# Batches 2 to 5 of a fused attention and expert kernel get new slots, and two product phases are interleaved

## The chip, the cores and the metric

The kernel runs on one core of one Trainium2 chip. The metric is the device time of one execution in microseconds (us), lower is better. PE is TensorE, ACT is ScalarE, DVE is VectorE, POOL is GpSimd and SP is SyncE.

## What is computed

Attention with a causal window of 64 positions over 8 batches and 8 heads of 576 positions and 64 dimensions, then two matrix products with `h - tanh(h)` between them.

```
scores = q @ k^T / sqrt(64);  mask = (0 <= i - j < 64)
attn   = softmax(where(mask, scores, -1e9)) @ v
x      = attn, heads side by side: [4608 tokens, 512]
h      = x @ w_in                  # [4608, 2048]
out    = (h - tanh(h)) @ w_out     # [4608, 512], float32
```

## The kernel before, in words

**Attention.** A batch b has four pairs of heads, numbered g = 4b to 4b+3. Each pair has nine tiles j of 64 queries and 128 keys. Its steps are these:

- `load` and `load_all` (lines 97 and 103) bring q and k from DRAM on POOL's queue, as one pair or as all eight heads of a batch; `load_v_all` (146) brings V into `vall`, of which there is one buffer.
- `cast` (86) brings a pair's rows into the order that PE takes, on DVE or POOL, in three row buffers each for q and k. `tr` (267) transposes them on PE through PSUM bank 3. For q, ACT copies one half out and then DVE the other; for k, ACT copies all of it.
- `scores` (334) makes three tiles in PSUM bank 4, and ACT takes the exponential (336). `masking` (340, DVE) sets the hidden part to zero. In batches 0 and 1 `tile_scores` (306) and `tile_pv` (322) do it for 64-column halves.
- `cast_v` (86) puts V into `vb`, of which there is one buffer. `keys_v` and `windows_v` (176, 161) move it to `vw`, nine DMAs for a batch, each of which a tile j needs.
- `tile_pv` (20 matmuls of 65 columns, banks 6 and 7; 322 to 328) or `pv` with `norm` (9 matmuls of 130 columns, banks 5 to 7; 346 to 357) makes the product with V and divides by the sums, into `xs`.
- `x_tr` (363) transposes `xs` on PE, with a copy by DVE or ACT; `x_dma` (378) does it with two transposing DMAs on SP's queue. Either fills `xT`, the input of the products.

**Products.** The 4608 tokens are nine chunks c of 512. `hp_mm` (393) makes one 128x512 block m of h for a chunk with four matmuls, ACT takes tanh (398) and `g_sub` (405, DVE) subtracts into `gT`. `yp_mm` (417) adds four of the sixteen blocks m into a 128x512 part of the output; after four calls `y_out` (422) copies it by ACT and SP stores it. A chunk c needs the attention of batch c and of the end of batch c-1.

**The order is written by hand.** `OPS` gives each slot 0 to 319 one product step: chunk 0's h in slots 0 to 30, its y in 32 to 47, chunk 1's h in 48 to 63 (the first three blocks together in slot 48), its y in 64 to 79, chunk 2's h in 80 to 95, and from slot 96 on h of chunk c in even slots and y of chunk c-1 in odd ones. `at(h, step, ...)` puts an attention step behind the product step of slot h. The last loop emits slot after slot, so each engine's instruction order follows from the slots, and within a slot from the order of the `at` calls. An engine and a DMA queue take their instructions in that order. `pace(h)` makes POOL wait for the `gT` block that precedes slot h, and so holds back the loads behind it. A DMA queue type has eight semaphores in turn, so the ninth DMA that POOL issues waits until the first has landed.

Batch 2 is in slots 47 to 79 in the kernel before, batch 3 in 62 to 95, and batches 4 and 5 follow with eight slots for a pair. The helper `std` places batches 2 and 3; both use `scores`, `masking`, `tile_pv` and `x_tr`.

Of the kernel before, what the change touches and what calls it, by code (L numbers as in the profile page):

```python
# [10 lines left out]
ACT = mybir.ActivationFunctionType  # L11
# [4 lines left out]
def kernel(  # L16
# [9 lines left out]
    nc = tc.nc  # L26
    B, H, S, D = q.shape
    NP = H // 2
    NJ = S // 64
# [6 lines left out]
    WPC = TOK // 64  # L36
    NC = NT // TOK
    M = d_ff // 128
    scale = 1.0 / (D ** 0.5)
# [16 lines left out]
    ps = psum.tile([128, 8, 512], F32, name="ps")  # L56

    ident = const.tile([128, 128], BF16, name="ident")
    tick = const.tile([1, 1], BF16, name="tick")
# [3 lines left out]
    hide = const.tile([128, 2, 64], BF16, name="hide")  # L63
# [3 lines left out]
    NR, NPT = 2, 4  # L67
# [5 lines left out]
    PT = [const.tile([128, NJ, 128], BF16, name=f"pt{i}") for i in range(NPT)]  # L73
    kT = [const.tile([128, 64 + S], BF16, name=f"kt{i}") for i in range(NR)]
    qT = [const.tile([128, 2, S], BF16, name=f"qt{i}") for i in range(NR)]
# [6 lines left out]
    def move(eng, o, i):  # L82
        if eng is nc.scalar:
            nc.scalar.activation(o, i, ACT.Copy)  # L84
        else:
            eng.tensor_copy(o, i)  # L86
# [70 lines left out]
    def windows_v(b, j, eng):  # L157
        if j == 0:
            keys_v(b, 0, eng)
        else:  # L160
            eng.dma_start(out=vw[b % 2][:, j].rearrange("p h c -> p (h c)"),  # L161
                          in_=vb[8 * j - 8:8 * j + 8].rearrange("p e h c -> p e (h c)"))
# [7 lines left out]
    def cast_v(b, pr, eng=nc.gpsimd):  # L170
        move(eng, vb[:, :, 2 * pr:2 * pr + 2, 0:D].rearrange("p e h d -> p h e d"),
             stage.pop((b, pr, "v")).rearrange("p h (e d) -> p h e d", d=D))

    def keys_v(b, j, eng=nc.sync):

        eng.dma_start(out=vw[b % 2][64:128, j].rearrange("p h c -> p (h c)"),  # L176
                      in_=vb[8 * j:8 * j + 8].rearrange("p e h c -> p e (h c)"))
# [12 lines left out]
    def load_w_in(i):  # L190
        nc.gpsimd.dma_start(out=w_in_sb[i], in_=w_in_r[:, :, 1024 * i:1024 * i + 1024])

    def w_in_tile(ki, m):
        i = m // 8
        f = 512 * (m // 4 % 2) + m % 4
        return w_in_sb[i][:, ki, f:f + 4 * 127 + 1:4]
# [45 lines left out]
    def chunk_tile(c):  # L242
        if c not in xT:
            xT[c] = xt_pool.tile([128, WPC, 2, 128], BF16, tag="xT", name="xT")
        return xT[c]
# [140 lines left out]

    def hp_mm(c, ms, split):

        outs = [ps[:, m % 3 if c < 3 else m % 2, :] for m in ms]
        for kis in ((0, 2), (1, 3)) if split else ((0, 1, 2, 3),):  # L390
            for m, hp in zip(ms, outs):
                for ki in kis:
                    nc.tensor.matmul(hp, w_in_tile(ki, m),  # L393
                                     chunk_tile(c)[:, :, ki % 2, 64 * (ki // 2):64 * (ki // 2) + 64],
                                     start=(ki == 0), stop=(ki == 3))
        for m, hp in zip(ms, outs):
            th = sm_pool.tile([128, TOK], F32, tag="th", name="th")
            nc.scalar.activation(th, hp, ACT.Tanh)  # L398
            HID[c, m] = hp, th
# [5 lines left out]
        nc.vector.tensor_tensor(gT[c][:, m, :], hp, th, ALU.subtract)  # L405

    def yp_bank(c, s):
        if c < 2:
            return (1, 2)[s % 2]
        return (0, 2)[s % 2] if c == NC - 1 else 2  # L410

    def yp_mm(c, st):
        s, part = divmod(st, 4)
        yp = ps[:, yp_bank(c, s), :]
        for i in range(4):
            m = 4 * part + i
            nc.tensor.matmul(yp, gT[c][:, m, s * 128:(s + 1) * 128], w_out_sb[:, m, :],  # L417
                             start=(m == 0), stop=(m == M - 1))
# [7 lines left out]
    OPS = {}  # L426
    for m in range(M):
        OPS[2 * m] = "h", 0, m
        OPS[32 + m] = "y", 0, m
        OPS[48 + m] = "h", 1, m  # L430
        OPS[64 + m] = "y", 1, m
        OPS[80 + m] = "h", 2, m
        for c in range(3, NC):
            OPS[32 * c + 2 * m] = "h", c, m
            OPS[32 * c + 2 * m + 1] = "y", c - 1, m
        OPS[32 * NC + 2 * m + 1] = "y", NC - 1, m
# [3 lines left out]
    def at(h, fn, *args):  # L440
        items.setdefault(h, []).append((fn, args))
# [16 lines left out]
    V, A, G, Y = nc.vector, nc.scalar, nc.gpsimd, nc.sync  # L458
# [22 lines left out]
    copy_mask()  # L481
    tile_scores(0, 0, (0, 1))
    tile_scores(0, 1, (4, 5))
    for j in range(NJ):
        keys_v(0, j, G)
    load_w_in(0)
    load_w_in(1)
    load_w_out(0)
# [35 lines left out]

    at(33, lambda: [cast_v(1, pr, V) for pr in range(NP)])
    at(34, more_constants)
    at(35, lambda: [keys_v(1, j, G) for j in range(NJ)])
    at(35, load, 7, "q", G)
    at(35, load_v_all, 2)
    for g in 8, 9, 10, 11:  # L530
        at(35, load, g, "k", G)
        at(35, load, g, "q", G)
    at(36, cast_pair, 4, V)
    at(37, tr_rows, 4, "k", 3, V)
    at(38, tr_rows, 4, "q", 0, A)
# [25 lines left out]
    at(47, x_tr, 1, 1, 0, 4, 3, V)  # L561
    at(47, x_tr, 1, 1, 4, 9, 6, A)

    for pr in range(NP):
        at(48, cast_v, 2, pr, G)
    at(49, lambda: [windows_v(2, j, G) for j in range(NJ)])
    at(49, load_v_all, 3)
    for g in range(12, 16):
        at(50, load, g, "k", G)
        at(50, load, g, "q", G)  # L570
    for i in range(2):
        at(140 + 4 * i, more_zeros, i)

    def std(g, ck, cq, t, tk, ss, ms, p):
        at(cq, cast, g, "q", V if g not in (10, 11, 15) else G)
        at(ck, cast, g, "k", V if g not in (10, 11, 15) else G)
        at(t, tr, g, "q", 3, A, V)
        at(tk, tr, g, "k", 3, A)
        for i in range(3):
            at(ss + 2 * i, scores, g, i, 4)  # L580
        at(ms, masking, g)
        at(p, tile_pv, g, (6, 7))

    for i, g in enumerate(range(8, 12)):
        a = (50, 55, 60, 65)[i]
        lead = 3 if i < 2 else 5
        std(g, a - lead + 1, a - lead, a, a + 2, a + 3, a + 8, a + (12 if i == 0 else 11))
    at(70, x_tr, 2, 0, 0, 4, 3, V)
    at(71, x_tr, 2, 0, 4, 9, 3, A)
    at(78, x_tr, 2, 1, 0, 4, 3, V)  # L590
    at(79, x_tr, 2, 1, 4, 9, 3, A)

    for g in range(3 * NP, B * NP):
        b, pr = divmod(g, NP)
        a = 8 * g - 48 - (0, 2, 4)[min(b - 3, 2)]
        s = 32 * b - (0, 2, 4)[min(b - 3, 2)]
        cv, ky = s - 72 + 5 * pr, s - 54
        if b == 3:
            a = (68, 73, 78, 82)[pr]
            cv = 62 + pr  # L600
        elif b == 4:
            a = 84 + 7 * pr
            cv, ky = 75 + 3 * pr, 86
        elif b == 5:
            cv, ky = 95 + 4 * pr, 108
        at(cv, cast_v, b, pr)
        if b == 3:
            lead = 3 if pr < 3 else 6
            std(g, a - lead + 1, a - lead, a, a + 2, a + 3, a + 8, a + 11)
            if pr == 0:  # L610
                for j in range(NJ):
                    at(67, windows_v, b, j, Y)
            if pr % 2:
                at(a + 12, x_tr, b, pr // 2, 0, 4, 3, V)
                at(a + 13, x_tr, b, pr // 2, 4, 9, 3, A)
            continue
        if b < 7:
            at(a - 7, cast, g, "q")
            at(a, tr, g, "q", 3, A, V)
        else:  # L620
            at(a - 14, cast_q, g)
            at(a - 12, bounce, g, "q")
            at(a - 6, tr_dma, g, "q")
        if b < 7:
            at(a - 5, cast, g, "k")
            at(a + 2, tr, g, "k", 3, A)
        else:
            at(a - 13, cast, g, "k")
            at(a - 11, bounce, g, "k")
            at(a - 5, tr_dma, g, "k")  # L630
        for i in range(3):
            at(a + 5 + 2 * i, scores, g, i, 4)
        at(a + 11, masking, g)
        for i in range(3):
            at(a + 13 + i, pv, g, i)
        at(a + 15, norm, g)
        if pr == NP - 1:
            at(a + 16, x_dma, b)
        for j in range(NJ):
            if pr == 0:  # L640
                at(ky + (j // 2 if b > 5 else 0), windows_v, b, j, Y)
        if pr == 0:
            if b > 3:
                hq, hk = s - (60 if b < 7 else 68), s - (64 if b < 7 else 72)
                hv = {4: 69, 5: 92}.get(b, s - 78)
                if b < 6:
                    hk, hq = {4: (71, 72), 5: (86, 89)}[b]
                for h, f in (hv, (load_v_all, b)), (hq, (load_all, b, "q")), (hk, (load_all, b, "k")):
                    at(h, pace, h)
                    at(h, *f)  # L650

    for h in range(32 * NC + 32):
        op = OPS.get(h)
# [2 lines left out]
        if op and op[0] == "h":  # L656
            c, m = op[1:]
# [43 lines left out]
```

## Time and profile before

| | |
|---|---|
| median of 13 runs (lowest, highest) | 353.16 us (351.33, 355.26) |
| time of the profiled execution | 353.05 us |
| its span | 351.3 us |
| PE busy in the span | 321.8 us, 2452 matmuls |
| DVE, ACT, POOL busy | 201.1, 185.1, 113.0 us |
| one h or y step of four matmuls, back to back | 0.86 us |
| POOL copies, `cast` and `cast_v` | 0.82 and 1.05 us |
| DMAs, median to landing: vw, vall, kall (8 heads), xT | 4.0, 11.2, 7.9, 3.6 us |

A busy PE is not PE at its peak, since the ends of matmuls are modelled. So PE is read by the steps from one start to the next: back to back a 512-column matmul takes 216 ns, a 128-column one 56 ns, one of 130 columns 57 ns, of 96 columns 42 ns and of 65 columns 22 ns. What a step takes beyond that is lost time.

### The profile page before, as it was taken

The numbers are of one execution on the slowest core, as the hardware profiler recorded it, in microseconds if no ns is written. First come the engines' busy times: TensorE is split into PE (matmuls) and PEld (weight loads), VectorE is DVE, ScalarE is ACT, GpSimd is POOL, SyncE is SP. The second block draws the span as 40 slices with busy tenths as digits, with TensorE's granted clock in tenths as the row PEclk, the third lists the DMA queues.
The fourth block names the chain that finished last, engine by engine and source line by source line (L and its number), as shares of the span: only waits on it lengthen the run. The fifth ranks groups of instructions, "written<-read, shape, count | busy, mean of one in ns | idle before, by whom it ended". The sixth has DMA issues, their size and how long they took to land.

```text
span 351.3 us, 6289 instructions
## 1 busy us (share of the span) xinstructions
PE 321.8 (92%) x2452; PEld 175.3 (50%) x2452; DVE 201.1 (57%) x336; ACT 185.1 (53%) x336; POOL 113.0 (32%) x169
## 2 busy tenths in 40 slices
PE   7889989794999869799899999999999999999994
PEld 3654544452455545455555555555555444444442
DVE  4565666883565567577766667666656344444300
ACT  3635534583545768467566666655554444444411
POOL 8850166684722612372272554610000000000000
PEclk9999999998799999999999999999999999999999
DMA  8999999989399179428498689689831400110021
GB/s 162 144 182 214 195 163 150 176 139 158 49 158 239 43 114 152 71 48 135 105 165 162 97 151 191 115 166 208 189 65 47 113 30 30 51 41 30 32 90 61
DMA packets 51399, 42.39 MB, mean 121 GB/s; under 512 B 21177, under 2 KB 44665, under 8 KB 51369
## 3 DMA queue, kind: packets, MB, share of 16 engines
q0 software_dynamic: 21728, 20.40, 38.7%
q1 hardware_dynamic: 29432, 21.30, 26.3%
q8 instruction: 19, 0.31, 0.4%
q10 hardware_dynamic: 208, 0.29, 0.3%
q14 instruction: 12, 0.09, 0.1%
HBM read 36.70 MB, written 11.21 MB: 136 GB/s over the span
## 4 chain that ended last, share of the span: by engine, by line
PE 68%; DMA 15%; POOL 7%; DVE 3%; ACT 3%; issue 2%; POOLq 0%; ACTq 0%; DVEq 0%
PE ps L417 31%; PE ps L393 27%; DMA vall<-in_v_dram 14%; PE ps L334 3%; PE ps L267 3%; PE ps L346 2%; POOL vw L176 2%; DMA kall<-in_k_dram 1%; POOL vb L86 1%; POOL vw L161 1%; DVE gT L405 1%; PE ps L322 1%; ACT pt L336 1%; POOL vall L154 1%; DVE qt L86 1%
## 5 line engine op out<-in xcount | busy, mean ns | idle before, releaser
L393 PE MATMUL ps<-xT,wi 128*128 128x512 bf16 x576 | 146.8, 385 | 2.6 <-DVE gT L405 2.5
L405 DVE TENSOR_TENSOR gT<-ps,th 128x512 bf16<-128x512 f32 x144 | 98.8, 691 | 82.6 <-ACT th L398 80.7
L417 PE MATMUL ps<-w_out_sb,gT 128*128 128x512 bf16 x576 | 143.8, 379 | 0.0
L398 ACT ACTIVATE th<-ps 128x512 f32<-128x512 f32 x144 | 85.7, 598 | 75.8 <-PE ps L393 74.3
L393 PEld LDWEIGHTS <-wi 128*128 128x128 bf16 x576 | 61.9, 114 | 51.0 <-issue 6.5
L417 PEld LDWEIGHTS <-gT 128*128 128x128 bf16 x576 | 53.3, 98 | 53.9 <-issue 0.2
L336 ACT ACTIVATE pt<-ps 128x384 bf16<-128x384 f32 x72 | 35.3, 490 | 31.7 <-PE ps L334 31.5
L86 POOL COPY vb<-vall 72x1024 bf16<-72x1024 bf16 x24 | 24.8, 1051 | 30.9 <-DMA vall<-in_v_dram 15.3
L422 ACT ACTIVATE ysb<-ps 128x512 f32<-128x512 f32 x36 | 21.6, 600 | 18.6 <-PE ps L417 18.6
L86 DVE COPY qt<-ps 64x576 bf16<-64x576 bf16 x20 | 15.2, 760 | 22.1 <-ACT qt L84 22.1
L334 PE MATMUL ps<-qt,kt 128*128 128x128 bf16 x216 | 24.1, 221 | 1.8 <-ACT pt L336 1.4
L357 DVE TENSOR_TENSOR xs<-ps,rc 64x576 bf16<-64x576 f32 x32 | 24.2, 755 | 0.8
L334 PEld LDWEIGHTS <-kt 128*128 128x128 bf16 x216 | 16.2, 98 | 12.0 <-issue 2.3
L340 DVE TENSOR_TENSOR pt<-pt,ps 128x1152 bf16<-128x1152 bf16 x24 | 17.9, 744 | 1.1 <-ACT pt L336 1.1
L346 PEld LDWEIGHTS <-pt 128*128 128x128 bf16 x144 | 12.0, 98 | 12.5 <-issue 1.3
L346 PE MATMUL ps<-vw,pt 128*128 128x130 bf16 x144 | 16.0, 220 | 1.0 <-DVE xs L357 1.0
L97 POOL DMA_DIRECT2D qall<-in_q_dram x15 | 9.7, 649 | 19.3 <-DMA vall<-in_v_dram 11.0
L86 POOL COPY qb<-qall 96x768 bf16<-96x768 bf16 x15 | 12.4, 826 | 10.9 <-DMA qall<-in_q_dram 7.1
L84 ACT ACTIVATE qt<-ps 64x576 bf16<-64x576 bf16 x20 | 12.7, 635 | 5.8 <-PE ps L267 5.8
L86 POOL COPY kb<-kall 96x768 bf16<-96x768 bf16 x19 | 15.6, 824 | 0.0
L267 PE MATMUL ps<-ident,qb 96*128 96x96 bf16 x120 | 8.6, 209 | 6.3 <-POOL qb L86 5.1
L84 ACT ACTIVATE kt<-ps 128x576 bf16<-128x576 bf16 x20 | 13.0, 648 | 1.4 <-PE ps L267 1.4
(74 smaller groups left out, 216.6 us busy)
## 6 DMA issues: line engine op xcount, KB each, us to landing
out_dram<-ysb SPq DMA_DIRECT2D x36, 256.0 KB, 2.2
vw<-vb SPq DMA_DIRECT2D x40, 130.0 KB, 4.0
vall<-in_v_dram POOLq DMA_DIRECT2D x7, 576.0 KB, 11.2
kall<-in_k_dram POOLq DMA_DIRECT2D x4, 576.0 KB, 7.9
qall<-in_q_dram POOLq DMA_DIRECT2D x4, 576.0 KB, 8.2
kall<-in_k_dram POOLq DMA_DIRECT2D x15, 144.0 KB, 10.3
qall<-in_q_dram POOLq DMA_DIRECT2D x15, 144.0 KB, 9.9
wi<-in_moe_w_in_dram POOLq DMA_DIRECT2D x2, 1024.0 KB, 11.6
```

The lines of the kernel that those rows point to most:

```text
L84: nc.scalar.activation(o, i, ACT.Copy)
L86: eng.tensor_copy(o, i)
L267: nc.tensor.transpose(tp[:, e, :], src[:, e, :], ident[:P, :P])
L334: nc.tensor.matmul(sp[:, i, :], kT[g % NR][:, 64 * j:64 * j + 128], qT[g % NR][:, :, 64 * j:64 * j + 64], start=True, stop=True)
L336: nc.scalar.activation(PT[g % NPT][:, 3 * grp:3 * grp + 3, :], sp, ACT.Exp, scale=scale)
L346: nc.tensor.matmul(ps[:, 5 + grp, 130 * i:130 * i + 130], PT[g % NPT][:, j, :], vw[b % 2][:, j, 2 * pr:2 * pr + 2, :], start=True, stop=True)
L357: nc.vector.tensor_tensor(xo[r, :, :, pr, :], ov[r, :, :, h, 0:D], rc[r].to_broadcast([64, 3, 3, 64]), ALU.mult)
L393: nc.tensor.matmul(hp, w_in_tile(ki, m), chunk_tile(c)[:, :, ki % 2, 64 * (ki // 2):64 * (ki // 2) + 64], start=(ki == 0), stop=(ki == 3))
L398: nc.scalar.activation(th, hp, ACT.Tanh)
L405: nc.vector.tensor_tensor(gT[c][:, m, :], hp, th, ALU.subtract)
L417: nc.tensor.matmul(yp, gT[c][:, m, s * 128:(s + 1) * 128], w_out_sb[:, m, :], start=(m == 0), stop=(m == M - 1))
L422: nc.scalar.activation(ysb, ps[:, yp_bank(c, s), :], ACT.Copy)
```

## The change

1. Chunk 1's y and chunk 2's h are interleaved in slots 64 to 95, as all later chunks are. Phases of h alone end with chunk 1's. `hp_mm` of chunk 2 has two PSUM banks in place of three, and y of chunk 1 has bank 2 alone in place of 1 and 2. Chunk 2's h begins at slot 66 (slot 80 before), so batch 2 has slots 47 to 65.
2. Batch 2 has its scores from `hidden_scores`: a 128x384 matmul of `ident` and `hide` puts the mask into the bank ahead of the three score matmuls, in banks 4 and 5 in turn, and `masking` is left out. Its casts move (pair 8 on DVE, 9 to 11 on POOL), its `cast_v` moves from POOL to DVE at slot 49, its `windows_v` from POOL's queue to SP's at slot 50.
3. Batch 3 goes through the loop of the later batches: `pv`, `norm` and `x_dma` (slot 92) in place of `tile_pv` and `x_tr`; its q and k come with `load_all` at slot 52, V at 53.
4. Batches 4 to 6 get new slots for loads, `cast_v` and `cast`. `windows_v` is spread, two DMAs to a slot. For batch 5, `behind_x(3)` makes POOL wait for the last of `x_dma(3)` ahead of each load.
5. Four of the nine `keys_v` of batch 0 go to SP's and ACT's queues, four of batch 1 to SP's. `load_v_all(2)` goes behind the loads of pair 8.

```
-        outs = [ps[:, m % 3 if c < 3 else m % 2, :] for m in ms]
+        outs = [ps[:, m % 3 if c < 2 else m % 2, :] for m in ms]
...
-        if c < 2:
+        if c == 0:
             return (1, 2)[s % 2]
...
-        OPS[64 + m] = "y", 1, m
-        OPS[80 + m] = "h", 2, m
+        OPS[66 + 2 * m if m < 15 else 95] = "h", 2, m
+        OPS[63 + 2 * m if m > 1 else 64 + m] = "y", 1, m
...
-    for j in range(NJ):
-        keys_v(0, j, G)
+    for j, eng in enumerate((Y, A, G, Y, A, G, G, G, G)):
+        keys_v(0, j, eng)
...
-    at(35, lambda: [keys_v(1, j, G) for j in range(NJ)])
+    at(35, lambda: [keys_v(1, j, (G, Y)[j % 2]) for j in range(NJ)])
...
-    for pr in range(NP):
-        at(48, cast_v, 2, pr, G)
-    at(49, lambda: [windows_v(2, j, G) for j in range(NJ)])
-    at(49, load_v_all, 3)
-    for g in range(12, 16):
-        at(50, load, g, "k", G)
-        at(50, load, g, "q", G)
+    def hidden_scores(g, grp, bank):
+        sp = ps[:, bank, 0:384].rearrange("p (i q) -> p i q", i=3)
+        nc.tensor.matmul(sp, ident, hide.rearrange("p h t -> p (h t)").unsqueeze(1).to_broadcast([128, 3, 128]),
+                         start=True, stop=False)
+        for i in range(3):
+            j = 3 * grp + i
+            nc.tensor.matmul(sp[:, i, :], kT[g % NR][:, 64 * j:64 * j + 128], qT[g % NR][:, :, 64 * j:64 * j + 64],
+                             start=False, stop=i == 2)
+        nc.scalar.activation(PT[g % NPT][:, 3 * grp:3 * grp + 3, :], sp, ACT.Exp, scale=scale)
+
+    at(47, cast_pair, 8, V)
+    at(48, cast_pair, 9, G)
+    at(49, lambda: [cast_v(2, pr, V) for pr in range(NP)])
+    at(50, lambda: [windows_v(2, j, Y) for j in range(NJ)])
+    at(50, cast_pair, 10, G)
+    at(52, cast_pair, 11, G)
+    at(52, load_all, 3, "k")
+    at(52, load_all, 3, "q")
+    at(53, load_v_all, 3)
+    for i, (g, p) in enumerate(((8, 58), (9, 59), (10, 61), (11, 63))):
+        at(48 + 3 * i, tr, g, "q", 3, A, V)
+        at(49 + 3 * i, tr, g, "k", 3, A)
+        for j in range(3):
+            at(50 + 3 * i + j, hidden_scores, g, j, 4 + (3 * i + j) % 2)
+        at(p, tile_pv, g, (6, 7))
+    at(62, x_tr, 2, 0, 0, 4, 4, V)
+    at(62, x_tr, 2, 0, 4, 9, 5, A)
+    at(65, x_tr, 2, 1, 0, 4, 3, V)
+    at(65, x_tr, 2, 1, 4, 9, 4, A)
...
+    def behind_x(b):
+
+        last = ((b + 1) * NJ - 1)
+        nc.gpsimd.tensor_copy(tick, chunk_tile(last // WPC)[0:1, last % WPC, 0, 0:1])
+
+    LOADS = {4: (63, 64, 72), 5: (96, 99, 102), 6: (124, 128, 114)}
...
+        a = 8 * g - 52
+        s = 32 * b - 4
...
-            a = (68, 73, 78, 82)[pr]
-            cv = 62 + pr
+            a = (62, 67, 72, 76)[pr]
+            cv, ky = 63 + pr, 67
         elif b == 4:
-            a = 84 + 7 * pr
-            cv, ky = 75 + 3 * pr, 86
+            a = (80, 87, 95, 102)[pr]
+            cv, ky = 77 + 3 * pr, 88
         elif b == 5:
-            cv, ky = 95 + 4 * pr, 108
+            cv, ky = 107 + 2 * pr, 114
+        elif b == 6:
+            cv = 120 + 4 * pr
...
-                at(ky + (j // 2 if b > 5 else 0), windows_v, b, j, Y)
+                at(ky + j // 2, windows_v, b, j, Y)
...
+            hk, hq, hv = LOADS.get(b, (s - 72, s - 68, s - 78))
+            if b == 3:
+                continue
+            for h, f in (hv, (load_v_all, b)), (hq, (load_all, b, "q")), (hk, (load_all, b, "k")):
+                at(h, pace, h)
+                if b == 5:
+                    at(h, behind_x, 3)
+                at(h, *f)
```

In the changed kernel's order SP takes, around slot 92, `windows_v(4)` j = 0 to 7, then the two DMAs of `x_dma(3)`, then `windows_v(4)` j = 8; around slot 118 the same with `windows_v(5)` and `x_dma(4)`.

More of the change, by code (lines that the diff above doesn't have):

```diff
@@ L526 @@
     at(34, more_constants)
-    at(35, lambda: [keys_v(1, j, G) for j in range(NJ)])
+    at(35, lambda: [keys_v(1, j, (G, Y)[j % 2]) for j in range(NJ)])
     at(35, load, 7, "q", G)
-    at(35, load_v_all, 2)
     for g in 8, 9, 10, 11:
@@ L532 @@
         at(35, load, g, "q", G)
+        if g == 8:
+            at(35, load_v_all, 2)
     at(36, cast_pair, 4, V)
@@ L571 @@
+    at(62, x_tr, 2, 0, 0, 4, 4, V)
+    at(62, x_tr, 2, 0, 4, 9, 5, A)
+    at(65, x_tr, 2, 1, 0, 4, 3, V)
+    at(65, x_tr, 2, 1, 4, 9, 4, A)
     for i in range(2):
         at(140 + 4 * i, more_zeros, i)
[L574 to L591, printed above, removed]
+    def behind_x(b):
+        last = ((b + 1) * NJ - 1)
+        nc.gpsimd.tensor_copy(tick, chunk_tile(last // WPC)[0:1, last % WPC, 0, 0:1])
+    LOADS = {4: (63, 64, 72), 5: (96, 99, 102), 6: (124, 128, 114)}
@@ L593 @@
     for g in range(3 * NP, B * NP):
         b, pr = divmod(g, NP)
-        a = 8 * g - 48 - (0, 2, 4)[min(b - 3, 2)]
-        s = 32 * b - (0, 2, 4)[min(b - 3, 2)]
+        a = 8 * g - 52
+        s = 32 * b - 4
         cv, ky = s - 72 + 5 * pr, s - 54
         if b == 3:
-            a = (68, 73, 78, 82)[pr]
-            cv = 62 + pr
+            a = (62, 67, 72, 76)[pr]
+            cv, ky = 63 + pr, 67
         elif b == 4:
-            a = 84 + 7 * pr
-            cv, ky = 75 + 3 * pr, 86
+            a = (80, 87, 95, 102)[pr]
+            cv, ky = 77 + 3 * pr, 88
@@ L604 @@
         elif b == 5:
-            cv, ky = 95 + 4 * pr, 108
+            cv, ky = 107 + 2 * pr, 114
+        elif b == 6:
+            cv = 120 + 4 * pr
         at(cv, cast_v, b, pr)
[L607 to L616, printed above, removed]
@@ L617 @@
         if b < 7:
-            at(a - 7, cast, g, "q")
+            at(a - {3: 4, 5: 4}.get(b, 7), cast, g, "q")
             at(a, tr, g, "q", 3, A, V)
@@ L624 @@
         if b < 7:
-            at(a - 5, cast, g, "k")
+            at(a - {3: 3, 5: 6}.get(b, 5), cast, g, "k")
             at(a + 2, tr, g, "k", 3, A)
@@ L640 @@
             if pr == 0:
-                at(ky + (j // 2 if b > 5 else 0), windows_v, b, j, Y)
+                at(ky + j // 2, windows_v, b, j, Y)
         if pr == 0:
[L643 to L650, printed above, removed]
+            hk, hq, hv = LOADS.get(b, (s - 72, s - 68, s - 78))
[6 more added lines that the diff above has]
+                at(h, *f)
     for h in range(32 * NC + 32):
```

## The prediction

> **What bounds the kernel now.** I read the page's busy times and slices first, then PE's steps by stretch, then its waits, then the queues behind the longest wait. The page's lines:
>
> ```profile
> span 351.3 us, 6289 instructions
> ...
> PE 321.8 (92%) x2452; PEld 175.3 (50%) x2452; DVE 201.1 (57%) x336; ACT 185.1 (53%) x336; POOL 113.0 (32%) x169
> ...
> PE   7889989794999869799899999999999999999994
> ...
> PEclk9999999998799999999999999999999999999999
> ```
>
> PE is the bound, and full from about 180 us on (the right half of its row). Its 2452 matmuls at their back-to-back steps (216 ns for 512 columns, 56 for 128, and so on) sum to 303.6 us. The last one starts at 345.2 us, so 41.5 us are lost: 19.4 up to 67.5 us, where slot 48 begins, 22.1 between there and 180, none after. Who ended the waits from 66 to 144 us, longest first:
>
> ```profile
> PE ps L267 <- POOL qb L86: 5.1, 1, 5.1
> PE ps L363 <- DVE xs L328: 1.8, 2, 1.2
> PE ps L334 <- ACT pt L336: 1.4, 3, 0.6
> ```
>
> One wait is large; the rest are many small ones behind copies. POOL's timeline says why that cast was late:
>
> ```profile
> 80.45 0.63 POOL L97 DMA_DIRECT2D kall<-in_k_dram  x1
> 85.83 0.63 POOL L97 DMA_DIRECT2D qall<-in_q_dram  x1 [4.75 <-DMA vall<-in_v_dram]
> 86.45 0.83 POOL L86 COPY qb<-qall 96x768 bf16<-96x768 bf16 x1
> ```
>
> The ninth load waits for the eighth before it, batch 3's V, and pair 10's cast stands behind it in order. The stages around it (span, then busy times by engine, granted clock, DMA share):
>
> ```profile
> 82.20:87.40 5.20, 0.09 (x2) 0.06 (x2) 0.36 (x1) 0.88 (x2) 1.57 (x3) 0.84 1.23 181
> 87.40:92.00 4.60, 4.60 (x34) 2.09 (x34) 2.15 (x3) 1.79 (x3) 4.60 (x6) 0.50 0.54 82
> ```
>
> PE is idle for 5.1 us and then runs 4.6 us at half clock, which loses another 2.3.
>
> [...] half clock from 2.9 us into the wait until 4.6 us after it. [...] a hardware queue doesn't escape a load on POOL's: SP's nine moves of V took 3.9 us to landing at 122 us with no load, and 8.4 at 94 us beside three loads (lines: both stretches, moves of V):
>
> ```profile
> DMA to landing us min/median/max: 3.7/3.9/4.4
> ...
> DMA to landing us min/median/max: 3.8/8.4/8.6
> ```
>
> [...] a DVE cast of 0.35 us took 1.49 at 67.8 us while POOL copied V.
>
> **The change part by part.** Times t count from the start of slot 48.
>
> *PE's program.* 12 hide matmuls of 384 columns (not in the trace; 384/512 of 216 ns = 162; 0.1 to 0.3 each bound it) +1.9; 18 transposes of 56 ns less, -1.0; 80 of 22 ns become 36 of 57, +0.3. Sum **+1.2**. Batch 2's four maskings of 0.74 leave DVE, which is not the bound: 0.
>
> *Front.* POOL issues four moves less ahead of the weights (4 x 0.57, and a 0.6 wait). [...] I take 1.5 us earlier for V of batch 1, not 2.9. PE waits 1.5 us at 47.8 for a cast behind that V (45.3). The two issues on ACT (0.43 each, by its first load) stand ahead of a copy that PE waits for, and give back 0.2 to 0.9. **-1.3** (-2.2 to +0.5).
>
> *Removed.* Slots 48 on are laid out anew, so all 22.1 us lost there go into the balance, 7.4 of them the long wait and its clock. What is late next:
>
> *A, slots 48 to 57, 4.6 us.* tr q and tr k of pair 8 share bank 3 with no matmul between (slots 49, 50 have none). q's two copies are 0.64 and 0.76 in series behind three tanh: PE finishes q at t = 2.9 and starts k at 4.9 (2.0 lost), then waits 0.6 for kt. DVE has four `cast_v` (0.36 each) ahead of `g_sub(1,1)`, beside POOL's two casts of pair 11, which wait for tr k of pair 8: some 1.3 for slot 52's bank. Smaller ones 0.7. PE then reaches slot 58 at t = 18.6 (11 steps of 0.86, eight hidden scores of 0.33, seven transposes of 0.26, plus 4.6).
>
> *B, slot 58, 4.7 us.* `tile_pv(8)` needs all nine moves of V. `cast_v(2)` ends at t = 8.3; POOL issues load_all(3) from t = 6.8, once pair 11 is cast, so moves and loads meet. Unloaded, nine moves took 121.99 to about 133.1 = 11.1 us: t = 19.4, a wait of 0.6. Loaded, 93.58 to about 110.2 = 16.6: t = 24.9, a wait of 6. I take 4.0, and 0.7 for the clock.
>
> *C, slots 59 to 66, 2.3 us.* y of chunk 1 now uses bank 2, freed by `g_sub(1,14)`, which stands behind tr q of pair 12 and two xT copies (1.3); h of chunk 2 directly behind the xT copies (0.55); rest 0.4. The 24 to 32 interleaved slots themselves have spare ACT and DVE time (0.60 and 0.69 per 1.73 us): 0 for two banks, else 0.3 a step.
>
> *D, slots 67 to 91, 2.6 us.* Slots 81 and 85 hold two `scores` in bank 4, each waiting for an exponential (0.6; in 81 also for a copy of pair 16: 1.2). 0.8 for V of batch 3 at slots 75 to 77, which is due within 1 us (0 to 4).
>
> *E, slot 95, 5.5 us.* SP takes the last move of `windows_v(4)` behind `x_dma(3)`:
>
> ```profile
> 174.66 2.84 SPq L378 DMA_TRANSPOSE xT<-xs  x2
> ```
>
> From the end of pv(15,2): norm 2.0 (172.65 to 174.66 before), two transposing issues 2.9, landing 3.9 = 8.8 us. PE has four steps and four small groups until pv(16,2): 4.3. Wait **4.5**, and 1.0 of a possible 2.3 for the clock. xT lands at 5.4 and is hidden under that wait; without it h of chunk 3 waits 1.
>
> *F, slots 116 to 123, 5.8 us.* The same order with `x_dma(4)`. k, q and V of batch 5 are issued after `x_dma(3)`, near slots 95, 99 and 102; V (alone 7.4 at 140.3; 11.2 with moves beside it) lands 16 us after slot 96. POOL's order then puts four `cast_v` and two casts, 5.8 us: 22.3. Eight moves issue by 28, two transposes by 31, the last move lands at 34.8; PE is at pv(20,2) at 31: 3.8; 1.5 at pv(20,0) and (20,1), 0.5 elsewhere. Were V on time, norm(19) alone would leave 2.4.
>
> The sum A to F is 25.5, against 22.1 removed: +3.4. With +1.2 and -1.3: **+3.3** on a span of 351.3. The profiled execution took 353.05, near the median of 353.16, so about **356.5**.
>
> **Rivals.**
> 1. *The moves of V come in time* (slot 58): POOL's loads build up slowly and the nine moves run nearly alone. B is 0.6 (-4.1), E keeps its clock (-1.0), V of batch 5 lands 7.4 after its issue, F 3.0 (-2.8): **348.5**, faster. It decides at t = 18.6: if the ninth move has landed by about 20, this is the case. For it: SP issues every 0.55 us when free. Against: nine moves took 8.4 us each beside loads.
> 2. *POOL falls behind.* V loads of 11.2 us instead of 7.4 hold every cast behind them; slots 75 to 77 wait 3 more, slots 116 to 123 another 3 to 4: **363**.
> 3. *Nothing beside the long wait changes*, B and E cancelled by order: 353.05 - 7.4 + 1.2 = 347; it needs E absent, against SP's order, and is counted in rival 1.
>
> **Numbers.** Forecast 0.55, its own range 352 to 360; rival 1 0.30; rival 2 0.15. The range runs from 346 to 363 (rival 1 with a front of -2.2 and A 1 less, up to rival 2): B from 0.6 to 6, E's clock 0 to 2.3, F 2.4 to 8, front 2.7 wide. Measurement tells about 0.3%, 1.1 us, from no change. Faster: 0.26 of rival 1 and 0.03 of the forecast, 0.29; within: 0.12; slower: 0.59.
>
> **What would show it.** Right: no idle PE at 82 to 87 us and no half clock there; PE idle over 3 us behind vw at slot 58, and over 4 at pv(16,2) with SP's last move of batch 4 issued behind two transposes; the same at pv(20,2); PE gapless after slot 128. PE's wait at 47.8 gone shows the front. Wrong: the ninth move landing before slot 58, or tr k of pair 8 without a wait, each makes the sum too high; casts on POOL that end PE's waits at slots 67 to 116 make it too low.

## The result, and the profile after

| | before | after |
|---|---|---|
| median (lowest, highest) | 353.07 us (350.81, 357.49), 48 runs | 379.22 us (375.61, 383.21), 11 runs |
| ratio | 1 | 1.0724, 95% interval 1.0694 to 1.0755 |
| span of the profiled execution | 351.3 us | 376.1 us |

The change makes the kernel 7.2% slower. Here and below, medians are of all runs, and ratios leave out runs in a slow state (more than 1.5% above the fastest run of their kernel). The forecast was 356.5, its range ended at 363: the direction was right, the size was not. The page of the changed kernel:

```profile
span 376.1 us, 6190 instructions
...
PE 328.2 (87%) x2402; PEld 178.0 (47%) x2402; DVE 200.7 (53%) x330; ACT 184.2 (49%) x332; POOL 103.6 (28%) x153
...
PE   5779998575989579599948999999999999999996
...
PEclk9568999999899899999988999999999999999999
```

The one dip of PE at 82 to 87 us in the kernel before (the 4 in its 10th slice) is gone. Slice 8 has a 5 in place of a 7 (slots 48 to 50, in stage A of the prediction), and dips follow in slices 10, 14, 17 (a 5 each) and 21 (a 4), with an 8 of the clock row in or behind each of these four. PE's waits between 66 and 206 us say what they are:

```profile
PE ps L346 <- DMA vw<-vb: 13.9, 5, 3.7
PE ps L322 <- DMA vw<-vb: 4.6, 4, 2.2
PE ps L267 <- DVE qt L86: 3.0, 4, 1.9
```

18.5 us of waits end with a move of V (`vw<-vb`). The kernel before had no such wait in this stretch. V is late in four batches one after the other, each time at the first product with V of the batch: at slot 58 for batch 2, and at pv(12), pv(16) and pv(20) for batches 3, 4 and 5. (pv(12,2) stands for the third of the three groups of pair 12; groups count from 0.) PE's lost time (steps beyond their back-to-back length), cut at the first h of a chunk:

| lost us, from first h of chunk to the next | start to 0 | 0 to 1 | 1 to 2 | 2 to 3 | 3 to 4 | 4 to 5 | 5 to 7 | sum |
|---|---|---|---|---|---|---|---|---|
| before | 11.6 | 7.8 | 12.4 | 7.6 | 2.0 | 0.1 | 0.1 | 41.5 |
| after | 13.3 | 7.3 | 13.9 | 16.5 | 13.0 | 0.1 | 1.7 | 65.7 |

Chunk 2's h starts at another place of the program in the two kernels, so columns 1 to 2 and 2 to 3 are read together: 20.0 before, 30.4 after. With 1.2 us more of PE's program this is 25.4 us to the last matmul, against 24.8 in the spans.

The clock loses with it. Around the first wait for batch 3's V (span, busy times, granted clock):

```profile
120.00:125.91 5.91, 2.20 (x20) 1.24 (x19) 1.53 (x3) 1.50 (x3) 0.00 (x0) 1.00 0.84 169
125.91:130.80 4.89, 4.76 (x25) 2.55 (x25) 3.08 (x5) 2.42 (x5) 4.25 (x5) 0.65 0.15 54
```

PE has 2.20 us of work in the first 5.91, waits until V lands, and then works at a mean clock of 0.65. After the start of slot 48 there are five such intervals of 3.41 us at half clock, at 93, 127, 158, 192 and 199 us. A matmul of 512 columns takes 427 ns from start to start inside them and 216 outside (medians), and PE's steps inside each are 1.4 to 1.6 us longer than back to back.

The 5, 6 and 8 near the start of the clock row are another 20.5 us at half clock, before 32 us, which the profile of the kernel before doesn't have. They are not booked as a cost: the run e13 below, with the front of the kernel before, has 17.1 us of them, and up to the first h it loses no more than the kernel before does without them.

Why is batch 3's V late? POOL's timeline of the changed kernel:

```profile
93.81 1.05 POOL L86 COPY vb<-vall 72x1024 bf16<-72x1024 bf16 x1 [4.97 <-DMA vw<-vb]
94.80 0.83 POOL L86 COPY qb<-qall 96x768 bf16<-96x768 bf16 x1
104.90 0.18 POOL L452 COPY tick<-gT 1x1 bf16<-1x1 bf16 x1 [9.28 <-DVE gT L405]
105.14 0.78 POOL L103 DMA_DIRECT2D kall<-in_k_dram  x1
105.91 1.06 POOL L86 COPY vb<-vall 72x1024 bf16<-72x1024 bf16 x1
...
108.56 2.06 POOL L86 COPY vb<-vall 72x1024 bf16<-72x1024 bf16 x2
```

The first `cast_v` of batch 3 starts at 93.81, once V has landed (93.4) and the last move of batch 2 has left the one buffer `vb` (93.6), which is the wait named in the line. The other three stand behind `pace(63)`, one element copied to hold back batch 4's loads, which waits 9.28 us. The last cast ends at 110.6. SP's first move starts at 110.64, and batch 4's loads run beside the nine:

```profile
110.64 0.62 SPq L176 DMA_DIRECT2D vw<-vb  x1
111.36 4.26 SPq L161 DMA_DIRECT2D vw<-vb  x5
115.71 0.91 SPq L424 DMA_DIRECT2D out_dram<-ysb  x1
116.72 3.36 SPq L161 DMA_DIRECT2D vw<-vb  x3
```

### The profile page after: what moved, and what is told of

It is laid out like the page before. It is cut to its first block, busy times and chain, and to the rows that moved or that the text cites. A ratio compares the mean times of both kernels' runs of the same rounds, so it can differ in the third digit from the quotient of the medians.

```text
span 376.1 us, 6190 instructions
## 1 busy us (share of the span) xinstructions
PE 328.2 (87%) x2402; PEld 178.0 (47%) x2402; DVE 200.7 (53%) x330; ACT 184.2 (49%) x332; POOL 103.6 (28%) x153
## 4 chain that ended last, share of the span: by engine, by line
PE 59%; DMA 24%; DVE 8%; ACT 3%; POOL 3%; issue 2%; SPq 1%; DVEq 0%; ACTq 0%; POOLq 0%
PE ps L417 26%; PE ps L393 25%; DMA vw<-vb 12%; DMA kall<-in_k_dram 9%; PE ps L334 3%; PE ps L346 2%; PE ps L267 2%; DMA vall<-in_v_dram 2%; DMA kt<-kd 2%; DVE gT L405 1%; DVE vb L86 1%; DVE qt L86 1%; DVE xs L357 1%; POOL vw L176 1%; ACT th L398 1%
## 5 line engine op out<-in xcount | busy, mean ns | idle before, releaser
L393 PE MATMUL ps<-xT,wi 128*128 128x512 bf16 x576 | 151.6, 392 | 2.3 <-DVE gT L405 1.3
L336 ACT ACTIVATE pt<-ps 128x384 bf16<-128x384 f32 x60 | 29.4, 490 | 44.0 <-PE ps L334 44.0
L346 PE MATMUL ps<-vw,pt 128*128 128x130 bf16 x180 | 21.3, 222 | 16.2 <-DMA vw<-vb 13.9
L86 POOL COPY vb<-vall 72x1024 bf16<-72x1024 bf16 x20 | 20.8, 1057 | 37.5 <-DMA out_dram<-ysb 14.1
L357 DVE TENSOR_TENSOR xs<-ps,rc 64x576 bf16<-64x576 f32 x40 | 30.2, 755 | 1.0
L422 ACT ACTIVATE ysb<-ps 128x512 f32<-128x512 f32 x36 | 21.5, 598 | 18.5 <-PE ps L417 18.5
L346 PEld LDWEIGHTS <-pt 128*128 128x128 bf16 x180 | 15.0, 99 | 23.9 <-issue 6.9
L334 PE MATMUL ps<-qt,kt 128*128 128x128 bf16 x180 | 20.6, 225 | 3.2 <-DMA kt<-kd 1.4
L86 POOL COPY kb<-kall 96x768 bf16<-96x768 bf16 x23 | 19.2, 836 | 14.8 <-DMA kall<-in_k_dram 8.4
L86 POOL COPY qb<-qall 96x768 bf16<-96x768 bf16 x19 | 16.2, 852 | 13.7 <-PE ps L267 8.9
L84 ACT ACTIVATE qt<-ps 64x576 bf16<-64x576 bf16 x20 | 12.7, 635 | 3.7 <-PE ps L267 3.7
L322 PE MATMUL ps<-vw,pt 128*64 128x65 bf16 x240 | 8.0, 211 | 6.2 <-DMA vw<-vb 4.6
```

What stands on the lines that cost most here:

```text
L334: nc.tensor.matmul(sp[:, i, :], kT[g % NR][:, 64 * j:64 * j + 128], qT[g % NR][:, :, 64 * j:64 * j + 64], start=True, stop=True)
L336: nc.scalar.activation(PT[g % NPT][:, 3 * grp:3 * grp + 3, :], sp, ACT.Exp, scale=scale)
L346: nc.tensor.matmul(ps[:, 5 + grp, 130 * i:130 * i + 130], PT[g % NPT][:, j, :], vw[b % 2][:, j, 2 * pr:2 * pr + 2, :], start=True, stop=True)
L357: nc.vector.tensor_tensor(xo[r, :, :, pr, :], ov[r, :, :, h, 0:D], rc[r].to_broadcast([64, 3, 3, 64]), ALU.mult)
L393: nc.tensor.matmul(hp, w_in_tile(ki, m), chunk_tile(c)[:, :, ki % 2, 64 * (ki // 2):64 * (ki // 2) + 64], start=(ki == 0), stop=(ki == 3))
L422: nc.scalar.activation(ysb, ps[:, yp_bank(c, s), :], ACT.Copy)
```

## The experiments

The theory: four separate placements make V late: loads beside the moves (batch 2), a wait on POOL ahead of the casts (batch 3), a move behind two transposes in SP's order (batches 4 and 5), and a late load (batch 5). The rival: the interleaved phases lose the time by themselves (two banks for h, one for y), and the waits for V are only where it shows.

| run | us | ratio to before, interval |
|---|---|---|
| changed kernel | 379.22 | 1.0724, 1.0694 to 1.0755 |
| e1, ninth move ahead of the transposes | 375.67 | 1.0644, 1.0571 to 1.0718 |
| e2, loads apart from moves, batches 2, 3 | 374.05 | 1.0573, 1.0476 to 1.0669 |
| e3, casts of V ahead of POOL's wait | 373.88 | 1.0594, 1.0517 to 1.0670 |
| e5, these three | 361.86 | 1.0298, 1.0221 to 1.0375 |
| e6, batch 5's V loaded as before | 378.36 | 1.0679, 1.0557 to 1.0801 |
| e7, phases of one product as before | 384.20 | 1.0884, 1.0798 to 1.0970 |
| e10, dummies in the waits | 377.87 | 1.0688, 1.0598 to 1.0778 |
| e11, e5 and loads of batches 6, 7 moved | 369.24 | 1.0453, 1.0371 to 1.0534 |
| e4, before, two pairs' casts on DVE | 354.58 | 1.0075, 1.0001 to 1.0150 |
| e13, before, three edits | 348.05 | 0.9849, 0.9806 to 0.9892 |

**e1, SP's order.**

```
-                at(ky + j // 2, windows_v, b, j, Y)
+                at(ky + min(j // 2, 3), windows_v, b, j, Y)
```

> The changed kernel with one edit: the ninth move of V of batches 4 to 7 gets the slot of the eighth, so SP takes it ahead of the two transposing DMAs of the batch before. Theory (E and F are SP's order): the last move of batch 4 lands near 153 us, before PE is at pv(16,2), so the wait of 3.7 us and its half clock go and only about 1.5 us of waiting for xT is left; at pv(20,2) the wait of 2.8 goes, the two of 2.3 and 1.4 before it stay, because they hang on V's loads. Sum 7 to 8 us less: 371 to 372.5. Rival (the moves are late because of loads beside them, or the interleaved phases cost by themselves): the waits move to xT and to the eighth move, and less than 2 us are won.

The waits went as the theory says: at pv(16,2) none is left (0.7 for xT at the next h in its place), the wait of 2.8 us at pv(20,2) is gone, and the loss from chunk 3 to 4 fell from 13.0 to 7.3. But only 3 us came out, not the 7 to 8 expected, and the interval overlaps that of the changed kernel, so this gain is not clear of the noise. In the profiled execution PE ran at half clock for 6.8 us each from 66, 93 and 128 us and for 3.4 from 76, where the changed kernel, up to 150 us, has 3.4 at 93 and at 127 (3 us more lost from chunk 1 to 2, ahead of the edit; the mean granted clock of the two profiles is 0.932 and 0.950), and this wait, which the edit doesn't touch, stands in the tail (0.5 to 0.8 us twice in the changed kernel):

```profile
PE ps L334 <- DMA kt<-kd: 3.5, 1, 3.5
```

q of batch 7 landed 9.1 us after its issue in this run and 7.8 in the changed kernel; POOL, SP and PE take it in turn with no slack. So E and the last wait of F are shown to be SP's order by the trace. That the run's time hardly fell is put down to losses elsewhere, from one execution.

**e2, loads apart from the moves.**

```
-    at(52, load_all, 3, "k")
-    at(52, load_all, 3, "q")
-    at(53, load_v_all, 3)
+    at(46, load_all, 3, "k")
+    at(46, load_all, 3, "q")
+    at(57, pace, 57)
+    at(57, load_v_all, 3)
```

> The changed kernel with batch 3's k and q issued at slot 46 in place of 52 and its V held by POOL until slot 57, so that the nine moves of V of batch 2 meet no load of V and little of k and q. Theory (B is the loads beside the moves): the ninth move lands 11 us after the first issue in place of 16.4, near 89 us; the waits of 4.6 us at tile_pv(8) and the half clock after it go, 5.5 to 7 us; batch 3's V comes some 3 us later, which is hidden by the wait of its casts for slot 63. 372 to 374. Rival (the moves are slow by themselves, SP's issue or DVE's casts set them): the ninth lands within 1 us of 93.6 and the time stays within 1.5 us of 379.

In the changed kernel the three loads and the moves of V start together:

```profile
75.80 0.78 POOL L103 DMA_DIRECT2D kall<-in_k_dram  x1
76.58 0.94 POOL L103 DMA_DIRECT2D qall<-in_q_dram  x1
77.51 0.83 POOL L146 DMA_DIRECT2D vall<-in_v_dram  x1
77.93 6.30 SPq L161 DMA_DIRECT2D vw<-vb  x8
```

The result is as the theory says. PE's wait for V from 80 to 96 us (e2; the changed kernel has 4.6 in four waits there):

```profile
PE ps L322 <- DMA vw<-vb: 0.6, 1, 0.6
```

The half clock at 93 us is gone, and 13.9 lost from chunk 1 to 2 became 8.6. All of the gain stayed, 5.3 us by the ratios, a little less than the 5.5 to 7 expected.

**e3, casts of V ahead of POOL's wait.**

```
-            cv, ky = 63 + pr, 67
+            cv, ky = 63, 67
```

> The changed kernel with the four cast_v of batch 3 all at slot 63, ahead of the POOL instruction that waits there for a gT block. Theory (D is that wait on POOL: three of four casts of V stand behind it for 9 to 11 us): the last cast ends near 98 us in place of 110.6, the moves of batch 3 are issued from 99 to 107 us with no load beside the first of them, and the wait of 3.9 us at pv(12,2) and the half clock after it go, 5.5 to 6.5 us less: 372.5 to 374. The small waits of some 6 us between 113 and 152 us stay. Rival (SP holds the moves behind a store of y, or the loads of batch 4 make them slow whenever they start): pv(12,2) still waits 2 us or more and under 3 us are won.

SP's queue in e3, to be read beside the one above:

```profile
95.54 0.62 SPq L176 DMA_DIRECT2D vw<-vb  x1
96.25 4.84 SPq L161 DMA_DIRECT2D vw<-vb  x5
110.44 0.34 SPq L424 DMA_DIRECT2D out_dram<-ysb  x1
110.88 2.44 SPq L161 DMA_DIRECT2D vw<-vb  x3
```

Six moves are out 15 us earlier. The wait at pv(12,2) shrank from 3.7 to 0.6 us, its half clock went, and 16.5 lost from chunk 2 to 3 became 11.7. The rival had one thing right: the last three moves stand behind a store of y that waits until 110.4, which is what the 0.6 is. 4.6 us by the ratios, where 5.5 to 6.5 were expected; the trace shows 1.6 us more at batch 5 and 2.5 more in the tail.

**e5, the three at once.** The three diffs above.

> The changed kernel with the three edits of the first runs at once (ninth move of V ahead of the transposing DMAs, batch 3's loads apart from batch 2's moves, casts of V of batch 3 ahead of POOL's wait). Theory: the waits are separate, one to a batch, so the gains add, 5 for batch 2, 5 for batch 3 and 8 for batches 4 and 5, less 2 to 3 for the next latest steps: 361 to 364. Rival (the interleaved phases lose the time by themselves, and a wait that is taken away comes back in the next batch): 367 or more.

361.86: the gains add (15.0 us by the ratios, where the three runs by themselves sum to 12.7). Of the 18.5 us of waits for V, 3.2 are left, both at pv(20). The waits were separate, and nothing about the interleaving brings them back. The other 10 us or so stay. Counted as in the table of lost time, chunks 1 to 3 now lose 17.3 us, less than the 20.0 of the kernel before; what is left stands at batch 5 (chunk 3 to 4: 7.9 against 2.0) and in the tail (5.5 against 0.2, most of it the wait for `kt`), and in 1.2 us of PE's program.

**e6, batch 5's V as before.** Loads at 86, 89 and 92 without `behind_x`, casts from 95, moves from 108.

> The changed kernel with the loads, cast_v and windows_v of batch 5 in the slots they had before (loads at 86, 89 and 92, no wait for the transposed chunk ahead of them, casts of V at 95 to 107, moves from 108). Theory (F is that V of batch 5 is loaded too late to be moved before slot 118): the waits of 6.5 us at pv(20) and both half clocks go, 7 to 9 us less; the loads now run beside batch 4's moves, which gives back 1 to 3 at pv(16,2): 371 to 375. Rival (F comes from SP's order alone): the ninth move still stands behind two transposes in the code's order of slots only if the moves come after slot 116, so this run would win no more than the last wait, 3 to 4 us, and the moves of batch 4 lose as much: 378 to 380.

F is what the theory says: 0.6 is all that PE waits at pv(20), and for `masking` and not for V; 13.0 lost from chunk 3 to 4 became 2.8. But chunk 2 to 3 rose from 16.5 to 25.8, far beyond the 1 to 3 expected: PE waits 10.9 us for V at pv(16,2) in place of 3.7. SP's queue in the changed kernel, then in e6:

```profile
142.76 6.30 SPq L161 DMA_DIRECT2D vw<-vb  x7
150.66 2.92 SPq L378 DMA_TRANSPOSE xT<-xs  x2
154.10 0.60 SPq L161 DMA_DIRECT2D vw<-vb  x1
```

```profile
143.48 7.69 SPq L161 DMA_DIRECT2D vw<-vb  x7
151.37 9.37 SPq L378 DMA_TRANSPOSE xT<-xs  x2
161.27 0.61 SPq L161 DMA_DIRECT2D vw<-vb  x1
```

Beside the loads of q and V of batch 5, two transposing DMAs hold SP for 9.37 us in place of 2.92, and the ninth move behind them is issued 7 us later. So `behind_x` and the late load protect the transposes, and the price is V of batch 5. Either placement loses about the same: the time is in the rival's range, and batch 4's moves did lose as much as was won, though not because F is SP's order alone.

**e7, phases of one product as before.**

```
-        OPS[66 + 2 * m if m < 15 else 95] = "h", 2, m
-        OPS[63 + 2 * m if m > 1 else 64 + m] = "y", 1, m
+        OPS[64 + m] = "y", 1, m
+        OPS[80 + m] = "h", 2, m
```

(and the three and two banks of the kernel before)

> The changed kernel with the products of chunks 1 and 2 as before: y of chunk 1 in slots 64 to 79, h of chunk 2 in 80 to 95, with three and two PSUM banks; all else as in the changed kernel. Theory (interleaving is free, what loses time is where the moves of V and the loads are placed): only the wait of 1.5 us for bank 2 at slot 64 goes, the waits for V stay: 376.5 to 379. Rival (interleaving with two banks for h and one for y makes the small waits of 6 us between 113 and 152 us): these go as well: 371 to 374.

Only the wait of 1.5 us at slot 64 went; the run is 5 us slower, which neither expected. The rival falls. The small waits of slots 81 to 95 are there with the phases apart as well; from 130 to 155 us in e7:

```profile
PE ps L346 <- DVE pt L340: 1.4, 2, 0.8
PE ps L334 <- ACT pt L336: 1.3, 2, 0.7
PE ps L393 <- DVE gT L405: 1.0, 3, 0.4
PE ps L334 <- DVE qt L86: 0.6, 1, 0.6
```

Chunks 1 to 3 lose 32.9 us in place of 30.4: h of chunk 2 alone in slots 80 to 95 puts a tanh and a `g_sub` into each slot, and PE's h steps wait 5.3 us for DVE's `g_sub` between 66 and 206 us (1.3 in the changed kernel). Another 1.7 is lost at batch 5 and 2.6 in the tail. With this placement of the attention the interleaving gains, if anything.

**e10, dummies in the waits.** 14 matmuls of 512 columns ahead of the third group of pv(12), pv(16), pv(20), 8 ahead of the second of pv(20).

> The changed kernel with dummy matmuls of 512 columns on constants ahead of four waits: 14 ahead of the third group of pv(12), pv(16) and pv(20), 8 ahead of the second group of pv(20), so that PE is busy for 3.0 or 1.7 us of each wait. They add no work that the output needs, and their products are overwritten. The waits end when they ended before. Theory (each half clock of 3.41 us costs 1.5 us by itself, as the steps inside it show): four of the five intervals after slot 48 go, 4 x 1.5 = 6 less: 372 to 374. Rival (the time after the wait is bound by copies and DMAs, so a slow PE costs nothing): within 1.5 us of 379, or above it if the dummies outlast a wait.

Inconclusive. Of the three waits with dummies ahead of them, two lost their half clock (158 and 199 us). At pv(12,2) it stayed: the dummies ran without a gap until 125.4 us, PE still waited 1.7, and the clock fell at 128.0. The waits without dummies, at slot 58 and in the first group of pv(20), were followed by 6.8 us at half clock each. With 3.4 more at 66 us the profile has 20.5 us of it after 60 us, in place of 17.1. At pv(20) the dummies outlasted the wait. The run is 1.3 us faster, which is within the intervals. What a half clock costs rests on the lengths of PE's steps inside it.

**e11, two more placements.** e5, V of batch 6 loaded at slot 122, k and q of batch 7 at 142 and 146, its V at 151, with casts and moves moved to suit.

> The three edits of the earlier runs, and two more of placement: V of batch 6 loaded at slot 122 in place of 114, away from the moves of batch 5, and q and k of batch 7 loaded at 142 and 146 ahead of its V (151). Theory (V moves beside a load are what is left of F, 3.6 us of waits and 1.5 of clock; the tail of 3.8 us is the q load of batch 7 that lands with no slack): F to about 2 and the tail to 0.5, from 361.9 down to 353 to 356. Rival (the moves and loads of batch 6 now meet instead, at pv(24), or batch 7's V comes late): 358 to 362.

Worse than e5 by 5.5 us by the ratios, beyond the rival. The load of V of batch 6 now starts 2.0 us ahead of `x_dma(4)`, and k of batch 6 just behind it:

```profile
173.48 3.25 SPq L161 DMA_DIRECT2D vw<-vb  x3
176.82 10.52 SPq L378 DMA_TRANSPOSE xT<-xs  x2
```

Two transposes again, 10.52 us; k of batch 6 took 15.3 us to landing (6.3 in the changed kernel). It is the finding of e6 a second time: in this kernel a load belongs neither beside the moves (nine took 16.4 us for batch 2, and 11.1 with no load in the kernel before) nor beside the transposes (9.4 and 10.5 us, where 2.9 without), and there is little room between. The other placement failed too: k, q and V of batch 7 now met one another (12.4, 15.4 and 20.9 us to landing), and the wait for `kt` in the tail was 5.5 us, 3.6 in e5.

**e4, e8, e12, e13, the kernel before.** Its one long wait stood behind POOL's casts of pairs 10 and 11. Can it go without the change?

```
-        at(cq, cast, g, "q", V if g not in (10, 11, 15) else G)
-        at(ck, cast, g, "k", V if g not in (10, 11, 15) else G)
+        at(cq, cast, g, "q", V if g != 15 else G)
+        at(ck, cast, g, "k", V if g != 15 else G)
```

> The kernel before with one edit: the casts of pairs 10 and 11 go to DVE in place of POOL. It asks what the wait of 5.1 us at 82 to 87 us cost, which the change removes: if it is POOL's order alone, that wait and its half clock (2.3) go, and something on DVE comes some 1 us later (a cast of 0.4 us in front of a g_sub): 346 to 348. Rival (what the cast stood behind, V of batch 3 and the loads, ends the next wait as well, at the casts of V of batch 3 on POOL): 350 to 353.

The wait and its half clock went (12.4 us lost from chunk 1 to 2 became 6.6), and the time did not: this execution lost 3.6 more ahead of slot 48 and 3.4 more in the tail, which the next three runs took on. e8 loads q and k of batch 7 four slots earlier:

> The kernel before with the casts of pairs 10 and 11 on DVE, and q and k of batch 7 loaded four slots (3.5 us) earlier. Theory (the wait of 5.1 us and its half clock were gone with the casts alone, but 2.2 us came back at 242 us because q of batch 7 landed 1.8 us later than in the kernel before, with no slack behind it): the wait for kt at 242 us goes, 350 to 352.5, unless POOL's casts of V meet DVE's maskings at 63 to 68 us again (4 us, which stays to chance). Rival (the tail hangs on SP's order of the two bounces, not on the load): the wait stays, 354 to 355.

Its 20 runs lie between 345.7 and 361.9, median 354.1, so no gain is shown; k now met V of batch 7, and k and q took 10.5 and 12.8 us to landing. e12 loads them six slots earlier and V after them:

> The kernel before with the casts of pairs 10 and 11 on DVE, and q and k of batch 7 loaded six slots earlier, ahead of its V, which is loaded later (151) and cast and moved in slots 162 to 174. Theory: the wait of 5.1 us with its half clock is gone (5.8 us by the trace of that edit alone), and with k and q loaded without V beside them the tail has slack again: 346 to 349. Rival (POOL's casts meet DVE's maskings at 63 to 68 us, or V of batch 7 comes late): 352 to 355.

The tail is gone: PE loses nothing after 180 us. But 20 runs spread from 345.6 to 358.2, median 352.6 (only the lowest few are near 346, so I don't take a ratio from those). In the profiled one, DVE's timeline has two maskings that take 0.91 us in the kernel before:

```profile
63.41 5.10 DVE L313 TENSOR_TENSOR pt<-pt,mask_sb 128x640 bf16<-128x640 bf16 x2
```

They met POOL's four casts of V (64.21 to 68.23 us), and PE waited 3.3 us for them. In the kernel before, the long wait at 82 us would cover such a delay, since its end is set by a load and not by PE; that is argued, for no trace of it has the slow maskings, and none of a run near 346 us was taken. e13 takes one part of the change and puts these casts on DVE at slot 49:

```
-        at(48, cast_v, 2, pr, G)
+        at(49, cast_v, 2, pr, V)
```

> The kernel before with three edits: casts of pairs 10 and 11 on DVE, q and k of batch 7 loaded ahead of its V, and now the four cast_v of batch 2 on DVE at slot 49 (one part of the change) in place of POOL at slot 48. Theory (what is left in the two-edit version is that POOL's four casts of V, 4.0 us, meet DVE's two maskings of pair 7 in some executions, which then take 4.9 us in place of 0.9, and PE waits 3.4; in the kernel before the wait of 5.1 us at 82 us covers that): no wait for a masking at 68 us in any execution, 345 to 348 and the runs closer together than 345.6 to 358.2. Rival (DVE has no room for the casts of V between the g_sub of chunk 1, or another chain spreads the runs): 350 to 353 with as wide a spread.

348.05 us (346.37 to 350.19) against 354.18 in the same session: 1.5% faster than the kernel before, the best of all, with the runs close together (3.8 us between lowest and highest, where e12 has 12.6), though the median just misses the 345 to 348 expected. Maskings take 0.91 us in its trace, the four casts 1.42 on DVE, and lost time fell from 41.5 to 34.8 us.

## Why the prediction was wrong, step by step

| term | predicted | measured | what showed it |
|---|---|---|---|
| PE's program | +1.2 | +1.2 | the matmuls of both traces |
| Front | -1.3 | +1.2, see below | start of slot 48 |
| A, slots 48 to 57 | 4.6 | 5.3 | trace |
| B, slots 58 and 59 | 4.7 | 7.0 | e2 |
| C, slots 60 to 66 | 2.3 | 2.1 | trace |
| **D, slots 67 to 94** | **2.6** | **12.2** | e3, e7 |
| E, slots 95 to 97 | 5.5 | 5.6 | e1 |
| slots 98 to 115 | 0 | 0.8 | trace |
| F, slots 116 to 125 | 5.8 | 10.6 | e1, e6 |
| the rest | 0 | 1.8 | trace |

The measured terms are PE's lost time in the changed kernel's trace, each with the half clock behind it. From A on they sum to some 45 us, where 25.5 was predicted.

**D is the step that failed.** "0.8 for V of batch 3 at slots 75 to 77, which is due within 1 us (0 to 4)" was 4.3 us lost at the wait in slot 77 and 1.7 of clock behind it. The prediction gives no working for the 1 us. F follows POOL's order from load to last move; D names no instruction on POOL. There `pace(63)` stands between the first and the second cast, and POOL idles behind it until slot 63's h is done. The nine moves then ran beside three loads and took 15.3 us (110.6 to 125.9). e3 took away the wait on POOL alone, and 0.6 of the 3.7 us of waiting was left. The other half of D's miss, some 4 us, is the small waits. I took all 22.1 us lost in the kernel before out of the balance and put 1.8 of small ones back for these slots; the trace has 6.2, of the same kinds and sizes as in the kernel before. e7 shows that they don't hang on the interleaving. They end with copies, exponentials and maskings; no run tested what brings them along.

**The clock was mis-sized.** The terms hold 1.7 us for it (0.7 in B, 1.0 in E, none in D and F); the five intervals cost 7.5. The waits for V at slot 58, pv(12,2) and pv(16,2) brought one each, those at pv(20) two. The waits there were 4.6 us in four parts, 3.7, 3.7, 3.7 in two parts, and 2.8 us. No run separated this cost from the wait. The prediction also read the one half clock of the kernel before too short: it ran from 85.7 to 92.5 us, from 3.5 us into the wait until 5.2 after it, and not from 2.9 until 4.6.

**B's mechanism was right, its size low.** The moves met the loads and took 16.4 us (77.2 to 93.6), which is the loaded case of 16.6 and not the 4.0 us of wait that I chose between the two ends. Rival 1 had the ninth move landed by t = 20; it came at t = 24.9. e2 shows that the loads are the cause.

**E and F.** E was right to 0.1 us, and e1 shows SP's order as its cause. F's mechanism was right as well: V of batch 5 lands late and the ninth move stands behind two transposes (e1, e6). Its size lacked the clock (2.9), and the waits were placed otherwise: 3.7 us in the first group of pv(20), where 1.5 was predicted for two groups, and 2.8 at pv(20,2), predicted 3.8. V of batch 6 was loaded at 183 us just beside the moves, and the transposes took 4.7 us in place of 2.9; no run took this away by itself.

**Front.** PE's wait at 47.8 us is gone, but slot 48 starts at 68.7 us in place of 67.5. The two issues on ACT took 1.48 and 0.71 us, not 0.43, and the 1.5 us I took for V of batch 1 was an estimate. As a term the front can't be told from zero, though: nine profiles of kernels with the changed front (three of them with two loads issued earlier, at slot 46) have slot 48 at 66.1 to 68.7 us, mean 67.4. PE's last matmul in the kernel before starts at 346.6 us of the span; the prediction's 345.2 fits a count from PE's first matmul at 1.6, and its 41.5 us lost stand.

**Rivals.** Rival 2 (POOL falls behind, 363) came nearest: V's casts held on POOL are D, at one place of the two that it named and without the clock. What held three of them is `pace(63)` and not, as it said, a slow load alone (V of batch 3 took 15.9 us to landing). At its other place V of batch 5 took 7.2 us, so the load was not slow there. "PE gapless after slot 128" was wrong by 1.7 us: the tail waits for q and k of batch 7. In the ten profiles that load them in the old place, q takes 7.4 to 9.3 us to landing and the tail loses 0.1 to 1.7 us where q takes up to 7.8, and 3.4 to 5.8 where it takes 8.2 or more.

**What was removed.** The 5.1 us wait with its half clock was worth 5.8 us of lost time by e4, less than the 7.4 booked. The 3.6 us that e4 loses ahead of slot 48 are not in the profile of the kernel before, and the edit doesn't touch them; whether its long wait hides them in other executions, no trace shows.

## What to carry to other kernels

When a schedule is laid out anew, follow each queue that a late step depends on, instruction by instruction, from load to last move, and ask of each waiting instruction what stands behind it: here loads beside the moves, one paced load on POOL and two transposes on SP made V late in four batches. Two of the fixes were worth some 5 us each by themselves, the third some 3 within the noise, and the three together 15 of the 26 us. Take out of the balance only those small waits whose cause the change removes, since the others were still there after it. A wait that ends with a load may cover delays ahead of it, so that its removal shows a gain only after those are mended as well (e4 alone gained nothing; e13, with two further edits, 1.5%).

## What the runs showed of the hardware

- Two transposing DMAs on SP's queue: 2.9 us of issue with no load beside them, 4.7 beside one load of V (changed kernel, 190 us), 9.4 and 10.5 beside two loads (e6, e11). No run here shows what makes them longer.
- Two DVE maskings took 5.10 us beside POOL's four copies (e12), and 4.85 in e4, in place of 0.91 in the kernel before, where they ended at 64.63 us and POOL's copies began at 65.04. In e12 the second one took 4.6 us and ended after the last of the four copies. With the copies on DVE the maskings took 0.91 (e13).
- In the changed kernel PE's granted clock was 0.50 for 3.41 us each from 93.23, 127.36, 158.08, 192.22 and 199.04 us, and before slot 48 for 13.65 us from 7.89 and 6.83 us from 24.96. In the kernel before it was 0.50 for 6.83 us from 85.70, 3.47 us into the wait of 5.11.
- In the 3.41 us ahead of each of the five intervals after slot 48 PE was busy for 19, 39, 10, 6 and 26% (busy as the profile models it). The last of them came with a wait of 2.8 us, at pv(20,2). Of the runs only e10 set PE's work in the waits on purpose: the half clocks at 158 and at 199 us are not in its profile, the one at pv(12,2) is.
